# Chunked attention and a snake MLP: V loads of one batch split in two, its last units reordered, and fewer output matmuls beside the attention

## The chip, the cores and the metric

The kernel runs on one core of one Trainium2 chip. A core has five engines with their own instruction streams: TensorE (PE in the profile; its weight loads are listed as PEld), VectorE (DVE), ScalarE (ACT), GpSimd (POOL) and SyncE (SP). They meet through semaphores. The metric is device time in microseconds (us) of one execution; less is better.

## The reference

Two stages run one after the other. The first is attention over chunks: 4 batches, 8 heads, 768 positions, head size 64. Each chunk of 32 queries sees its own 32 keys, 16 to the left, 8 to the right and 8 memory keys.

```python
chunk, left_ctx, right_ctx = (32, 16, 8)
for c in range(nc):
    q_c = q[:, :, c_start:c_end].copy()
    k_full = np.concatenate([mem_k, k_ctx], axis=2)
    v_full = np.concatenate([mem_v, v_ctx], axis=2)
    scores = scale * np.matmul(q_c, k_full.transpose(0, 1, 3, 2))
    scores = scores - np.max(scores, axis=-1, keepdims=True)
    a = np.exp(scores)
    a = a / (np.sum(a, axis=-1, keepdims=True) + 1e-09)
    out[:, :, c_start:c_end] = np.matmul(a, v_full)
```

The second is an MLP over the 3072 tokens with 512 features, 2048 hidden ones:

```python
h = x @ w_in
s = np.sin(alpha * h)
g = h + s * s / (alpha + 1e-09)
out = (g @ w_out)
```

## The kernel before, in words

Work is staged by batch. For each batch of 768 tokens there is an attention stage and an MLP pass, and the output product of a batch is spread over the stages that follow.

**Attention.** Three chunks are taken together, so a batch has 8 groups of 96 queries, and a tile of 96 queries sees 128 columns. `qk` makes the scores `sc` of four head pairs with 8 small matmuls, `exps` turns them into `pt` on ScalarE with 3 to 4 Exp instructions, `pv` multiplies by V into `ot` (8 matmuls) and normalizes on VectorE (`rinv`, then `x_blk`), and `xt` transposes `x_blk` (4 matmuls) and copies the result into `xT`, the input of the MLP.

**Batch 0** runs in `first_burst`, from a list written by hand, `ORDER`. In it "k n" and "q n" transpose a head pair, "s n" is `qk` of unit n, "e n" its exponentials, "v n" its `pv`, "x n" its `xt`, and "z n" is n matmuls of zeros. Unit n holds four query groups of head pair n // 2; so units 4 and 5 read V of heads 4 and 5, units 6 and 7 that of heads 6 and 7. For units 2 to 7 `xt` puts 2 matmuls of zeros (`spin`) ahead of its transposes. After the exponentials of unit 7, line 375 does a one-column Sin on ScalarE whose result nothing reads.

**Batches 1, 2 and 3** run in `burst(b, stream, shares, lag)`. Step s issues `qk` and `exps` of group s, `pv` of group s - lag and `xt` of group s - lag - 1. Between them the step takes `shares[s]` output matmuls from a `Stream`. The stream holds the output product `l2` of the batch before: 96 matmuls of 128x512, in 6 groups of 16 with one output tile each; after a group the tile is copied by `put_out` (VectorE or ScalarE in turn) and sent out. `take(n)` adds n to a debt; it stops after a finished group, and what is left of the debt is taken by the next call.

**The MLP pass** goes over 16 column blocks ft. `l1` makes `hT` with 8 matmuls, then Sin on ScalarE (`u`), a square `s` on ScalarE, VectorE or GpSimd by a string of letters (A, D, P), and `finish` adds both on VectorE into `gT`. In the pass of batch 0 the stream is empty; after it, 4 output matmuls and then 3 after each of eight transposed pieces run ahead of the attention of batch 1. In the passes of batches 1 and 2, 2 output matmuls are taken from the stream ahead of each ft from 1 on, in that of batch 3 it is 3; in batches 1 and 2 every second ft also transposes a piece of K or Q of the next batch (`tt_a`). What is still in the stream when the last pass ends is done there.

**Buffers.** PSUM has a pool `big` of 3 tiles (`sc`, `ot`, `hT` and some transposes) and a pool `smp` of 2 (`o`, `z`, `tt_a`). A new tile waits for the last reader of the one whose place it takes.

**Loads.** Q, K, V and the weights are issued on GpSimd's queue. [...] a DMA is issued only when the one eight before it has landed. `load_v(b, n0, n1)` issues four DMAs for heads n0 / 8 to n1 / 8: 48 + 48 rows, and the left and right neighbours of each query group. Batch 0's V goes in three calls: heads 0 and 1 (n 0 to 16), heads 2 and 3, and heads 4 to 7; the weights `w_in` (four DMAs), K and Q of batch 1 and `w_out` follow.

Of the kernel before, what the change touches and what calls it, by code (L numbers as in the profile page):

```python
# [12 lines left out]
KW = 856  # L13
ORDER = (
    "k 0,q 0,memk 0,memv 0,k 1,s 0,e 0,z 1,s 1,e 1,q 1,k 2,s 2,e 2,s 3,v 0,q 2,e 3,k 3,x 0,v 1,q 3,s 4,e 4,x 1,"
    "s 5,e 5,z 1,v 2,s 6,e 6,z 2,v 3,x 2,v 4,s 7,e 7,x 3,v 5,x 4,v 6,x 5,v 7,x 6,x 7"
)
BF = mybir.dt.bfloat16
F32 = mybir.dt.float32
ACTF = mybir.ActivationFunctionType  # L20
# [29 lines left out]
def kernel(  # L50
# [12 lines left out]
    nc = tc.nc  # L63
# [25 lines left out]
    rows = consts.tile([P, 6], F32, name="rows")  # L89
# [36 lines left out]
    def load_v(b, n0, n1):  # L126


        vw = vws[b % 2].rearrange("p h j c -> p (h j) c")
        vf = v[b].rearrange("h s d -> (h s) d")  # L130
        vf = vf.rearrange("(n p) d -> p n d", p=QW)
        parts = (
            (vw[16:64, n0:n1, 0:D], vf[0:48, n0:n1]),
            (vw[72:120, n0:n1, 0:D], vf[48:96, n0:n1]),
            (vw[0:16, n0 + 1:n1, 0:D], vf[80:96, n0:n1 - 1]),
            (vw[120:128, n0:n1 - 1, 0:D], vf[0:8, n0 + 1:n1]),
        )
        for dst, src in parts:
            nc.gpsimd.dma_start(dst, src)  # L139
# [14 lines left out]
    zeros = consts.tile([P, 512], BF, name="zeros")  # L154
    nc.vector.memset(zeros[:], 0.0)  # L155

    def spin(n, z=None):

        if z is None:
            z = smp.tile([P, 512], F32, name="z", tag="sm")  # L160
        for _ in range(n):
            nc.tensor.matmul(z[:], zeros[:, 0:P], zeros[:])  # L162
# [26 lines left out]
        out=biasm[:], in0=rows[:, 0:5], scalar1=1.0, scalar2=-NEG, op0=ALU.subtract, op1=ALU.mult)  # L189
    nc.scalar.copy(memk_bf[:], memk_f[:])  # L190
    load_v(0, 16, 32)
    load_v(0, 32, 64)
    with nc.allow_non_contiguous_dma(reason="alpha transpose load"):
        nc.sync.dma_start(alpha_sb[:], moe_alpha.rearrange("(ft p) -> p ft", p=P))

# [81 lines left out]
    def exps(cells, sc):  # L277
        pt = pts[state["n"] % NPT]
        state["n"] += 1
        for m in range(3):  # L280
            cols = [((1 if j == 0 else 0), 4, (2 if j == NJ - 1 else 3))[m] for _, j in cells]
            c0 = 0
            for c1 in range(1, 5):
                if c1 < 4 and cols[c1] == cols[c0]:
                    continue
                nc.scalar.activation(  # L286
                    pt[:, 0:H * QW].rearrange("p (g e c) -> p e g c", g=4, e=2)[:, :, c0:c1, 32 * m:32 * m + 32],
                    sc[:, :, 0:4 * QW].rearrange("p g (e c) -> p g e c", e=4)[:, :, c0:c1, 32 * m:32 * m + 32],
                    ACTF.Exp, bias=biasm[:, cols[c0]:cols[c0] + 1], scale=0.125,
                )  # L290
                c0 = c1
        return pt
# [17 lines left out]
        )  # L310
        return x_blk, ot

    def xt(dst, x_blk, ot, copy=nc.vector.tensor_copy):
        if ot is None:
            z = smp.tile([P, 512], F32, name="z", tag="sm")
            spin(2, z)
            xtp = z[:].bitcast(BF)[:, 0:KT * QW]
        else:
            xtp = ot[:].bitcast(BF)[:, 0, 640:640 + KT * QW]
        xtp = xtp.rearrange("p (k c) -> p k c", k=KT)  # L320
        for kt in range(KT):
            nc.tensor.transpose(  # L322
                xtp[:, kt, :], x_blk[:, 2 * kt:2 * kt + 2, :].rearrange("p e d -> p (e d)"), ident[0:QW, 0:QW]
            )
        copy(dst, xtp)
# [4 lines left out]
    def burst(b, stream, shares, lag):  # L330

        xT = xp.tile([P, KT, S], BF, name="xT")
        ptl, xbl = {}, {}
        for s in range(NJ + lag + 1):
            n = shares[s] if s < len(shares) else 0
            if s < NJ:
                ptl[s] = exps(row(s), qk(row(s)))
            stream.take(n // 3, True)
            if 0 <= s - lag < NJ:
                xbl[s - lag] = pv(b, row(s - lag), ptl.pop(s - lag))  # L340
            stream.take((n + 1) // 3, True)
            if 0 <= s - lag - 1 < NJ:
                j = s - lag - 1
                xt(xT[:, :, QW * j:QW * j + QW], *xbl.pop(j))
            stream.take((n + 2) // 3, True)
        return xT

    def first_burst(kq):

        xT = xp.tile([P, KT, S], BF, name="xT")  # L350
        cells = [[(u // 2, 4 * (u % 2) + c) for c in range(4)] for u in range(8)]
        scl, ptl, xbl = {}, {}, {}
        for what, n in [t.split() for t in ORDER.split(",")]:
            n = int(n)
            if what == "k":
                t_k(kq[0], n)
            elif what == "q":
                t_q(kq[1], n, nc.vector.tensor_copy if n == 1 else nc.scalar.copy)
            elif what == "memk":
                mt = smp.tile([P, HP, 32], BF, name="mt", tag="sm")  # L360
                for hp in range(HP):
                    nc.tensor.transpose(
                        mt[:, hp, :],
                        memk_bf[0:32, 2 * hp:2 * hp + 2, :].rearrange("p e d -> p (e d)"),
                        ident[0:32, 0:32])
                nc.vector.tensor_copy(memkT[:], mt[:])
                put_memk(0)
            elif what == "memv":
                put_memv(0)
            elif what == "s":  # L370
                scl[n] = qk(cells[n])
            elif what == "e":
                ptl[n] = exps(cells[n], scl.pop(n))
                if n == 7:
                    nc.scalar.activation(rows[:, 0:1], zeros[:, 0:1], ACTF.Sin)
            elif what == "z":
                spin(n)
            elif what == "v":
                x_blk, ot = pv(0, cells[n], ptl.pop(n))
                xbl[n] = x_blk, (ot if n < 2 else None)  # L380
            elif what == "x":
                hf = n % 2
                xt(xT[:, n // 2, HALF * hf:HALF * hf + HALF].rearrange("p (k c) -> p k c", k=KT),
                   *xbl.pop(n), nc.scalar.copy if n in (4, 5, 6) else nc.vector.tensor_copy)
        return xT


# [106 lines left out]
    stream = Stream()  # L494
    xT = first_burst(kq)
# [3 lines left out]
    for i in range(B):  # L499
        gT = gp.tile([P, FT, S], BF, name="gT")  # L500
        last = i == B - 1
        at_ft = {2 * n: n for n in range(8)}
        pieces = []
        if not last:
            srcs = [(kq_next[n % 2], n // 2) for n in range(2 * HP)]
        state["pools"] = 1

        def pair_to(n):
            while len(pieces) < min(n, 2 * HP):
                pieces.append(pair_up(*srcs[len(pieces)], nc.vector.tensor_copy if i == 0 and len(pieces) in (2, 4, 6) else None))  # L510

        def piece(n):
            pair_to(n + 3)
            (t_k if n % 2 == 0 else t_q)(pieces[n], n // 2)

        if 0 < i < B - 1:
            pair_to(2)
        finish, late = None, None
        for ft in range(FT):
            sq = ("DADPADAPADAPDAAA" if i == 0 else "ADAAPDADADAPADAD")[ft]  # L520
            if 1 <= ft:
                stream.take(3 if last else 2)
            if 0 < i < B - 1 and ft in at_ft:
                piece(at_ft[ft])
            if i == 0 and ft == 8:
                pair_to(2)
            if i == 0 and ft == 13:
                load_v(1, 0, H * NJ)
            if finish is not None and ft - 1 == 11 and i == 0:
                late = finish  # L530
            elif finish is not None:
                finish()
                if late is not None:
                    late()
                    late = None
            finish = l1(i, ft, xT, gT, sq, i == 0 and ft in (3, 7, 11))
        finish()
        stream.add(l2(i, gT, last))
        if not last:
            if i == 0:  # L540
                state["pools"] = 0
                stream.take(4)
                for n in range(2 * HP):
                    piece(n)
                    stream.take(3, True)
                put_memv(1)
            if i + 2 < B:
                kq_next = load_qk(i + 2)
            if i == 0:
                xT = burst(i + 1, stream, (5, 5, 5, 4, 4, 4, 4, 4, 3, 3, 3, 3), 3)  # L550
            else:
                xT = burst(i + 1, stream, (16, 8, 6, 6, 6, 5, 5, 5, 5, 5), 1)
            if i + 2 < B:
                put_memk(i + 2)
            stream.take(3)
            if i + 2 < B:
                load_v(i + 2, 0, H * NJ)
                put_memv(i + 2)
# [31 lines left out]
```

The softmax here doesn't subtract the row's maximum and nothing guards it: scores larger than these inputs give would overflow.

## Time and profile before

The median of five runs is 233.96 us (233.74 to 234.1). The profiled execution took 234.1 us, and its span from the first to the last instruction is 232.3 us.

| Stage (us from the span's start) | length | PE busy | DVE busy | ACT busy |
|---|---|---|---|---|
| load and attention of batch 0 (0 to 27.8) | 27.8 | 23.3 | 18.4 | 17.3 |
| MLP pass of batch 0 (27.8 to 50) | 22.2 | 21.2 | 18.7 | 18.4 |
| transposes for batch 1 (50 to 59.5) | 9.5 | 9.0 | 8.4 | 5.0 |
| attention of batch 1 (59.5 to 78.3) | 18.8 | 17.9 | 12.9 | 14.4 |
| MLP pass of batch 1 (78.3 to 107) | 28.7 | 27.7 | 24.6 | 22.9 |
| attention of batch 2 (107 to 128.7) | 21.7 | 21.3 | 14.1 | 14.0 |
| MLP pass of batch 2 (128.7 to 158.5) | 29.8 | 29.0 | 24.9 | 24.1 |
| attention of batch 3 (158.5 to 179.8) | 21.3 | 21.0 | 13.4 | 13.4 |
| MLP pass of batch 3 (179.8 to 211.4) | 31.6 | 30.0 | 22.2 | 21.6 |
| output of batch 3 (211.4 to 232.3) | 20.9 | 17.7 | 2.5 | 1.5 |

Busy time is the time in which the engine had an instruction under way. Matmuls are pipelined, so PE counts as busy although it may issue less than it could. An engine's share is an average over stages; what bounds a stage is read from the wait that ends last in it.

### The profile page before, as it was taken

The numbers are of one execution on the slowest core, as the hardware profiler recorded it, in microseconds if no ns is written. First come the engines' busy times: TensorE is split into PE (matmuls) and PEld (weight loads), VectorE is DVE, ScalarE is ACT, GpSimd is POOL, SyncE is SP. The second block draws the span as 40 slices with busy tenths as digits, with TensorE's granted clock in tenths as the row PEclk, the third lists the DMA queues.
The fourth block names the chain that finished last, engine by engine and source line by source line (L and its number), as shares of the span: only waits on it lengthen the run. The fifth ranks groups of instructions, "written<-read, shape, count | busy, mean of one in ns | idle before, by whom it ended". The sixth has DMA issues, their size and how long they took to land.

```text
span 232.3 us, 4566 instructions
## 1 busy us (share of the span) xinstructions
PE 217.9 (94%) x1813; PEld 123.1 (53%) x1842; DVE 160.1 (69%) x288; ACT 152.6 (66%) x246; POOL 69.5 (30%) x80
## 2 busy tenths in 40 slices
PE   7996899989989999999999999998999999899994
PEld 2454565555446565654555656564555555453453
DVE  5675679888657897988467798887565368774110
ACT  3487789884887387898564877878664676880110
POOL 8898312595912115157300315020000020110000
PEclk9999999999999999999999999999999999999999
DMA  6999999999999910109995101010111010101112
GB/s 83 149 175 151 206 204 206 208 156 91 146 235 168 88 45 0 48 5 175 172 142 90 45 0 48 0 45 3 45 48 57 36 47 0 45 0 48 71 66 90
DMA packets 51805, 21.13 MB, mean 91 GB/s; under 512 B 36296, under 2 KB 48840, under 8 KB 51784
## 3 DMA queue, kind: packets, MB, share of 16 engines
q0 software_dynamic: 45568, 14.41, 76.1%
q1 hardware_dynamic: 6216, 6.43, 9.4%
q8 instruction: 14, 0.23, 0.4%
q14 instruction: 7, 0.06, 0.1%
HBM read 28.94 MB, written 6.29 MB: 152 GB/s over the span
## 4 chain that ended last, share of the span: by engine, by line
PE 61%; ACT 12%; DVE 9%; DMA 8%; issue 6%; POOL 2%; POOLq 1%; DVEq 0%; ACTq 0%
PE o L479 27%; PE hT L400 21%; DMA q_bf<-in_q_dram 5%; DVE gT L429 5%; ACT u L412 4%; PE ot L301 3%; ACT pt L286 3%; DMA vw<-in_v_dram 2%; PE sc L270 2%; DVE s L421 2%; ACT s L415 2%; PE tt_a L242 2%; PE ot L322 2%; PE o L468 2%; PE o L449 1%
## 5 line engine op out<-in xcount | busy, mean ns | idle before, releaser
L400 PE MATMUL hT<-xT,w_in_sb 128*128 128x384 bf16 x488 | 87.1, 326 | 3.0 <-DVE gT L429 2.8
L479 PE MATMUL o<-w_out_sb,gT 128*128 128x512 bf16 x313 | 84.9, 380 | 1.8 <-issue 0.5
L429 DVE SCALAR_TENSOR_TENSOR gT<-s,inv_alpha,hT 128x768 bf16<-128x768 f32 x61 | 61.0, 1012 | 19.7 <-ACT s L415 11.2
L412 ACT ACTIVATE u<-hT,alpha_sb 128x768 f32<-128x768 f32 x61 | 54.8, 898 | 24.5 <-PE hT L400 23.5
L400 PEld LDWEIGHTS <-w_in_sb 128*128 128x128 bf16 x512 | 49.3, 98 | 37.5 <-issue 3.8
L286 ACT ACTIVATE pt<-sc,biasm 128x256 bf16<-128x256 f32 (+2 forms) x104 | 39.1, 471 | 15.4 <-PE sc L270 15.4
L479 PEld LDWEIGHTS <-gT 128*128 128x128 bf16 x336 | 29.3, 98 | 24.3 <-DVE gT L429 1.2
L417 POOL TENSOR_TENSOR s<-u 128x768 f32<-128x768 f32 x9 | 13.2, 1466 | 87.5 <-ACT u L412 61.3
L415 ACT ACTIVATE s<-u 128x768 f32<-128x768 f32 x32 | 27.0, 844 | 1.0
L421 DVE TENSOR_TENSOR s<-u 128x768 f32<-128x768 f32 x23 | 24.3, 1056 | 2.3 <-ACT u L412 2.2
L306 DVE TENSOR_TENSOR x_blk<-ot,rinv 96x512 bf16<-96x512 f32 x32 | 22.0, 686 | 1.1
L139 POOL DMA_DIRECT2D vw<-in_v_dram x24 | 22.0, 924 | 0.6 <-DMA q_bf<-in_q_dram 0.5
L216 POOL COPY pr<-q_bf 128x768 bf16<-128x768 bf16 x12 | 10.8, 897 | 34.3 <-PE tt_a L242 24.4
L437 DVE COPY o_sb<-o 128x512 f32<-128x512 f32 x12 | 8.3, 689 | 15.6 <-PE o L479 15.5
L437 ACT COPY o_sb<-o 128x512 f32<-128x512 f32 x11 | 6.4, 584 | 17.9 <-PE o L479 17.9
L305 DVE RECIPROCAL rinv<-ot 96x8 f32<-96x8 f32 x32 | 6.4, 201 | 16.5 <-PE ot L301 16.3
L301 PEld LDWEIGHTS <-pt 128*128 128x128 bf16 x256 | 11.7, 97 | 7.5 <-issue 3.0
L301 PE MATMUL ot<-vw,pt 128*128 128x65 bf16 x256 | 13.0, 193 | 2.3 <-DMA vw<-in_v_dram 1.1
L162 PE MATMUL z<-zeros 128*128 128x512 bf16 x36 | 12.6, 451 | 2.1 <-DVE zeros L155 1.2
L242 PEld LDWEIGHTS <-pr 128*128 128x128 bf16 x144 | 10.0, 98 | 5.9 <-DVE pr L216 0.9
L270 PEld LDWEIGHTS <-kTi 64*128 64x128 bf16 x256 | 6.8, 94 | 11.3 <-PE ot L322 5.5
L322 PEld LDWEIGHTS <-x_blk 96*128 96x128 bf16 x128 | 8.7, 97 | 7.3 <-DVE x_blk L306 1.5
(76 smaller groups left out, 169.8 us busy)
## 6 DMA issues: line engine op xcount, KB each, us to landing
out_dram<-o_sb SPq DMA_DIRECT2D x23, 256.0 KB, 2.4
k_bf<-in_k_dram POOLq DMA_DIRECT2D x3, 768.0 KB, 8.7
q_bf<-in_q_dram POOLq DMA_DIRECT2D x3, 768.0 KB, 12.4
vw<-in_v_dram POOLq DMA_DIRECT2D x6, 384.0 KB, 15.0
w_in_sb<-in_moe_w_in_dram POOLq DMA_DIRECT2D x4, 512.0 KB, 9.7
w_out_sb<-in_moe_w_out_dram POOLq DMA_DIRECT2D x2, 1024.0 KB, 24.1
k_bf<-in_k_dram POOLq DMA_DIRECT2D x4, 192.0 KB, 5.1
q_bf<-in_q_dram POOLq DMA_DIRECT2D x4, 192.0 KB, 5.6
```

The lines of the kernel that those rows point to most:

```text
L139: nc.gpsimd.dma_start(dst, src)
L242: nc.tensor.transpose(t[:, r, :], src[:, r].rearrange("p e d -> p (e d)"), ident[:])
L286: nc.scalar.activation(pt[:, 0:H * QW].rearrange("p (g e c) -> p e g c", g=4, e=2)[:, :, c0:c1, 32 * m:32 * m + 32], sc[:, :, 0:4 * QW].re ...
L301: nc.tensor.matmul(otv[:, n // 4, n % 4, :], pt[:, QW * n:QW * n + P], vws[b % 2][:, 2 * hp + n % 2, j, 0:D + 1])
L306: nc.vector.tensor_tensor(out=x_blk[:].rearrange("p (g e) d -> p g e d", g=2), in0=otv[0:QW, :, :, 0:D], in1=rv.unsqueeze(3).to_broadcast( ...
L400: nc.tensor.matmul(hts[hf][:, 0:HALF], w_in_sb[:, kt, P * ft:P * ft + P], xT[:, kt, HALF * hf:HALF * hf + HALF], start=(kt == 0), stop=(kt ...
L412: nc.scalar.activation(u[:], hT[:, :, 0:HALF], ACTF.Sin, scale=alpha_sb[:, ft:ft + 1])
L415: nc.scalar.activation(s2[:], u[:], ACTF.Square)
L421: nc.vector.tensor_tensor(out=s2[:], in0=u[:], in1=u[:], op=ALU.mult)
L429: nc.vector.scalar_tensor_tensor(out=gv, in0=s2[:], scalar=inv_alpha[:, ft:ft + 1], in1=hT[:, :, 0:HALF], op0=ALU.mult, op1=ALU.add)
L437: (nc.vector.tensor_copy if s % 2 == 0 else nc.scalar.copy)(o_sb[:], o[:])
L479: nc.tensor.matmul(o[:], gT[:, ft, P * s:P * s + P], w_out_sb[:, ft, :], start=(ft == 0), stop=(ft == FT - 1),)
```

## The change

It does five things. (1) V of heads 4 to 7 of batch 0 is loaded by two calls, each of four DMAs, in place of one. (2) In `ORDER`, "s 7,e 7" stands ahead of "v 4". (3) `xt` puts 2, 2, 1, 1, 0, 0 matmuls of zeros ahead of the transposes of units 2 to 7 in place of 2 each, and the copy of unit 3 into `xT` is on ScalarE, not on VectorE. (4) The Sin of line 375 is gone. (5) The shares of the output matmuls in the attention of batches 1, 2 and 3 are smaller.

```diff
-    "s 5,e 5,z 1,v 2,s 6,e 6,z 2,v 3,x 2,v 4,s 7,e 7,x 3,v 5,x 4,v 6,x 5,v 7,x 6,x 7"
+    "s 5,e 5,z 1,v 2,s 6,e 6,z 2,v 3,x 2,s 7,e 7,v 4,x 3,v 5,x 4,v 6,x 5,v 7,x 6,x 7"
...
-    load_v(0, 32, 64)
+    load_v(0, 32, 48)
+    load_v(0, 48, 64)
...
-    def xt(dst, x_blk, ot, copy=nc.vector.tensor_copy):
+    def xt(dst, x_blk, ot, copy=nc.vector.tensor_copy, warm=0):
...
-            spin(2, z)
+            spin(warm, z)
...
                 ptl[n] = exps(cells[n], scl.pop(n))
-                if n == 7:
-                    nc.scalar.activation(rows[:, 0:1], zeros[:, 0:1], ACTF.Sin)
...
-                   *xbl.pop(n), nc.scalar.copy if n in (4, 5, 6) else nc.vector.tensor_copy)
+                   *xbl.pop(n), nc.scalar.copy if n in (3, 4, 5, 6) else nc.vector.tensor_copy,
+                   (0, 0, 2, 2, 1, 1, 0, 0)[n])
...
-                xT = burst(i + 1, stream, (5, 5, 5, 4, 4, 4, 4, 4, 3, 3, 3, 3), 3)
+                xT = burst(i + 1, stream, (5, 5, 4, 4, 4, 3, 3, 3, 3, 3, 2, 2), 3)
             else:
-                xT = burst(i + 1, stream, (16, 8, 6, 6, 6, 5, 5, 5, 5, 5), 1)
+                xT = burst(i + 1, stream, (16, 8, 6, 5, 5, 5, 5, 5, 4, 4), 1)
```

## The prediction

> **What bounds the kernel now.** The page's first part gives PE 217.9 of 232.3 us. Its fourth part, the chain that ended last, says who sets the end:
>
> ```profile
> PE 61%; ACT 12%; DVE 9%; DMA 8%; issue 6%; POOL 2%; POOLq 1%; DVEq 0%; ACTq 0%
> ```
>
> So an output matmul moved costs nothing only where it goes into a stretch in which PE is not that 61%. I went through the stages in order of time. First the chain in batch 0 (start, length, what):
>
> ```profile
> 10.31 6.18 DMA q_bf<-in_q_dram
> ...
> 16.77 5.67 DMA vw<-in_v_dram
> ...
> 22.58 0.40 PE ot L301 x8
> ...
> 23.30 1.36 ACT pt L286 x4
> ...
> 24.67 1.28 ACT L375
> ...
> 26.17 0.38 ACT xT L325
> ```
>
> The last V piece lands at 22.44; only then run v 4, s 7 behind it, e 7, the unused Sin's table load, and the xT copies on ACT; the MLP's first matmul is at 27.79. Who holds V back stands in POOL's timeline (start, length, idle before and its releaser):
>
> ```profile
> 11.13 5.14 POOL L139 DMA_DIRECT2D vw<-in_v_dram  x7
> 16.77 0.69 POOL L139 DMA_DIRECT2D vw<-in_v_dram  x1 [0.50 <-DMA q_bf<-in_q_dram]
> 17.84 3.01 POOL L202 DMA_DIRECT2D w_in_sb<-in_moe_w_in_dram  x4 [0.38 <-DMA vw<-in_v_dram]
> ```
>
> POOL issues one DMA per 0.6 to 0.75 us and waits for the DMA eight before. The issues by size and time to landing, in narrow windows, give
>
> ```profile
> vw<-in_v_dram POOLq DMA_DIRECT2D x1, 31.0 KB, 5.7
> vw<-in_v_dram POOLq DMA_DIRECT2D x1, 15.0 KB, 4.8
> w_in_sb<-in_moe_w_in_dram POOLq DMA_DIRECT2D x1, 512.0 KB, 6.6
> ```
>
> Then a step of batch 2's attention, on PE:
>
> ```profile
> 117.08 0.34 PE L270 MATMUL sc<-qT,kTi 64*128 64x96 bf16 x8
> 117.36 0.60 PE L479 MATMUL o<-w_out_sb,gT 128*128 128x512 bf16 x2
> 118.26 0.38 PE L479 MATMUL o<-w_out_sb,gT 128*128 128x512 bf16 x1
> 118.65 0.60 PE L479 MATMUL o<-w_out_sb,gT 128*128 128x512 bf16 x2
> ```
>
> PE has no gap over 0.1 us, ACT idles 0.4 to 0.9 us per step for sc: PE-bound. Last, the end of batch 3's pass, where the stream is empty:
>
> ```profile
> 201.48 0.89 ACT L412 ACTIVATE u<-hT,alpha_sb 128x768 f32<-128x768 f32 x1
> 202.44 1.47 POOL L417 TENSOR_TENSOR s<-u 128x768 f32<-128x768 f32 x1 [11.25 <-ACT u L412]
> 203.95 1.01 DVE L429 SCALAR_TENSOR_TENSOR gT<-s,inv_alpha,hT 128x768 bf16<-128x768 f32 x1 [1.09 <-POOL s L417]
> 205.01 2.81 PE L400 MATMUL hT<-xT,w_in_sb 128*128 128x384 bf16 x16 [0.27 <-DVE gT L429]
> ```
>
> Here PE waits for ACT, POOL and DVE in turn, through the hT buffers.
>
> [...] the trace agrees (5 o in 1.08 us of the chain, 0.216 each). [...] the page here shows PEclk 9 in all slices. [...] The trace is higher, 4.3 us for the first 192 KB and 4.8 for 15 KB with others in flight; I use the trace.
>
> **The change part by part.**
>
> *Split V.* The four DMAs of heads 4 and 5 go out at 13.79, 14.5, 15.2 and, since the fourth waits for Q's landing as now, 16.77. It carries 15 KB with half the V ahead of it: 4.8 to 5.7 us, landing 21.6 to 22.4, so v 4 gains 0.1 to 0.9. Heads 6 and 7 take w_in's place at 17.84, and at 0.73, 0.73 and 0.58 us per issue the last starts at 19.88; with 4.3 to 5.7 it lands at 24.2 to 25.6. I take 4.8, since less is queued ahead: v 6 starts at V = 24.75, against 24.65 now. The unknown is V.
>
> *Order.* s 7 follows x 2 at 21.5 instead of 22.91; its sc buffer is free. e 7 then ends near 23.3, not 24.66, so nothing waits on ACT after V.
>
> *After V.* x 5 (1 zero matmul), v 7 at V + 0.62; x_blk of 7 ends at V + 2.22 (rinv 0.2 and x_blk 0.69 twice on DVE, at today's offsets); x 7 at V + 2.35, the MLP at V + 2.52 = 27.27. Now it is V + 3.14, for the 0.69 wait for ACT and the zeros. The table load goes between x 6's copy (ends V + 2.35) and the first Sin: ends V + 3.65, and hT is complete at V + 3.98. Hidden; uncovered it would cost 1.28. First Sin: 28.8, not 29.30. **-0.5**; ends -1.0 (V 24.2) and +0.35 (V 25.6). The copy of unit 3 on ACT falls behind e 7, where ACT is idle. Six zero matmuls fewer (1.3 us) leave PE a gap of about 1 us near 24[...].
>
> The first w_in goes out at 20.5 instead of 17.84. At 6.6 us it would land at 27.1, just in time. Later loads slip by about 2 us: batch 1's K and Q (now 36.4 and 40.2; copied at 41.4 and 42.1, no one waiting before 50), w_out (45.3 for 50.2), V of batch 1 (60.5 for 64.7): slack. The pass of batch 0 follows ACT (16 Sins at 0.90 and 8 squares at 0.84 are 21.1 of the 22.9 us from the first Sin to the last square's end at 52.2), so it hands the gain on.
>
> *Batch 1.* The stream gives 6 matmuls fewer to the attention (47 to 41), and the pass gets them behind ft 9, 10 and 11 (18 to 24). From the table load at 60.51 the attention is ACT's: five Exp sets end at 67.87, then each step is sc to Exp to sc, 1.68 us, with PE equally full; last comes DVE at 1.11 us per group. So only about 0.25 of the 1.30 is got. In the pass DVE has a backlog from 94 to 110.2; the later hT of ft 12 (+0.87) delays its Sin, its square and the gT of ft 12 and 13, and the next sc waits for the latter: 107.2 instead of 106.7. **+0.25** together.
>
> *Batch 2.* By the order of instructions the attention has 64 instead of 70: -6 x 0.216 = -1.30, all PE-bound (shortest step 1.88, over ACT's 1.68). The pass has 32 instead of 26: 2 more behind ft 0, 2 each behind ft 13 and 14. The first cost 0.43; at the end PE now idles 0.58 for gT, which takes in most of the rest; next sc +0.64. **-0.65**. The 64th output copy now comes at the attention's very end; with the V memory cast 0.61 and the table load 1.28 the first Sin is 0.9 late, but hT 3 needs its gT 0.9 us after that is ready.
>
> *Batch 3.* Again -1.30. In the pass 2 more after ft 0, 1 more after ft 8, 3 more after ft 9. Sin 10 has to wait for hT 10, which comes 1.3 later, less ACT's queue: Sin 11 +1.2, POOL's square, gT 11, hT 14, gT 15 at 212.4 instead of 211.4: +1.03. **-0.27**; were the tail fully bound by PE it would be 0, with full cover -0.8.
>
> Sum: -0.5 + 0.25 - 0.65 - 0.27 = -1.17. The span 232.3 becomes 231.1, the profiled execution 234.1 becomes 232.9; the median, 0.14 lower, 232.8. Matmul records are partly missing and each tail was walked by hand, so I state 232.9.
>
> **Rivals.**
> A. The passes take back all that the attentions give. For it: batches 1 to 3 move 18 matmuls, 3.9 us, and PE's real slack at the ends of the three passes is only about 0.55, 0.58 and 0.88 us of named waits. Against: the pass of batch 1 has room for more fill, since DVE sets its end. With batch 0 also even (V at 25.3): 233.9.
> B. Slower: the first w_in lands late. Four more issues ahead of it on POOL put it at 20.5. For it: the four w_in DMAs took 6.6 to 12.5 us, median 9.7; at 9.7 it lands at 30.2 and the MLP starts 2.4 late instead of 0.5 early, all else as above: 235.7. Against: the long ones queued behind each other, the first took 6.6 with all of V ahead of it. It decides from a landing of 28.9 on (27.8 plus the 0.67 of batches 1 to 3 plus 0.47).
> C. More is won: V lands at 24.2 and the tails hide more (batch 1 at 0, batch 3 at -0.8): -1.0 - 0.65 - 0.8 = -2.45, 231.5.
> That the change does not do what it says is excluded by the order of instructions.
>
> **How the numbers follow.** Forecast 0.53, A 0.22, B 0.13, C 0.12. The forecast's own range is 232.2 to 233.6, from V (0.9 us wide) and 0.4 for each tail. For 8 in 10 I cut half of B and part of C: 231.7 to 234.6. A difference of 0.2%, 0.47 us, is about what this kernel's measurement can tell. Faster: 0.85 of the forecast, C and a little of A, 0.58; same: the rest of the forecast and most of A, 0.24; slower: B and some of A, 0.18.
>
> **What would show it.** First hT near 27.3 with v 6 waiting for vw until about 24.8; w_in not named as a releaser of PE; the attentions of batches 2 and 3 shorter by 1.3 each and that of batch 1 by 0.1 to 0.4; passes of batches 2 and 3 longer by 0.6 and 1.0; the table load ended before the first hT. The forecast is wrong if v 6 waits past 25.3, if hT waits for w_in, if PEclk dips below 9 before 30 us, or if the passes grow by 1.3 each.

## The result and the profile after

The changed kernel takes 236.82 us, median of 27 runs (233.92 to 239.74), against 233.97 us, median of 48 runs (233.16 to 234.81) of the kernel before. The medians differ by 2.85 us, 1.2%; the ratio is 1.006 (95% interval 1.0045 to 1.0075), and it is smaller than that of the medians because it leaves out the executions more than 1.5% above the fastest. The forecast was 232.9 us with a range up to 234.6: the change makes the kernel slower, not faster.

The times of after lie in steps, by the mean granted TensorE clock of the execution: ten runs with 1.0 take 233.92 to 235.84 us, ten with 0.993 take 236.16 to 238.52, five with 0.986 take 238.77 to 239.74; three in between, with 0.998 or 0.999, take 234.87 to 236.59 (28 executions: one of 235.84 us is listed with its clock besides the 27). A clock of 1.0 is full speed; in the trace of before, which has 0.998, the clock falls only in the last microsecond of the span, to 0.50 from 231.56 us on. The 13 executions with 0.998 or more have a median of 235.44 us, so after is 1.5 us slower than before even at full clock. The profiled execution took 238.52 us, span 236.7, clock 0.993.

The page of after: the chain's shares by engine, and the row of the granted clock in 40 slices of 5.9 us, in tenths of full speed (9 is 90% or more).

```profile
PEclk9999979999999999999999999999999999999999
PE 54%; DVE 12%; ACT 11%; DMA 9%; issue 7%; POOL 4%; POOLq 1%; DVEq 0%; ACTq 0%
```

Before, PE had 61% of the chain and DMA 8%. The 7 in the clock's row is the slice from 29.6 to 35.5 us. Now the chain of batch 0 (start, length, what):

```profile
10.09 7.04 DMA q_bf<-in_q_dram
17.13 0.28 issue
17.41 3.24 POOL vw L139 x5
20.65 8.04 DMA w_in_sb<-in_moe_w_in_dram
28.69 0.05 issue
28.74 5.70 PE hT L400 x24
```

Where it had run over V, v 4, e 7, the Sin's table load and the xT copies, it now runs from Q's landing over POOL's issues to the first w_in. POOL's timeline of after (start, length, idle before and its releaser):

```profile
10.93 4.68 POOL L139 DMA_DIRECT2D vw<-in_v_dram  x7
17.41 3.25 POOL L139 DMA_DIRECT2D vw<-in_v_dram  x5 [1.80 <-DMA q_bf<-in_q_dram]
20.65 3.03 POOL L203 DMA_DIRECT2D w_in_sb<-in_moe_w_in_dram  x4
```

and the issues from 16 to 24 us by size, number and time to landing:

```profile
vw<-in_v_dram POOLq DMA_DIRECT2D x2, 96.0 KB, 3.2
vw<-in_v_dram POOLq DMA_DIRECT2D x2, 15.0 KB, 3.1
vw<-in_v_dram POOLq DMA_DIRECT2D x1, 30.0 KB, 4.2
```

V is in sooner than forecast: the last piece, issued at about 20, landed near 24. These short landings fall where the DMA engines moved little: in the table of stretches 34 GB/s from 18 to 20 us, where before they moved 126. PE's timeline shows what it then waited for:

```profile
26.28 0.34 PE L323 MATMUL z<-ident,x_blk 96*128 96x96 bf16 x4 [0.49 <-DVE x_blk L307]
28.74 5.70 PE L400 MATMUL hT<-xT,w_in_sb 128*128 128x384 bf16 x24 [2.12 <-DMA w_in_sb<-in_moe_w_in_dram]
```

x 7 is done at 26.6 and the MLP could start. It waits 2.12 us for w_in, and then 24 matmuls take 5.5 us up to the next ones, which before took 3.91. The same 5.6 us in the table of stretches (PE, PEld, DVE, ACT, POOL busy; PEclk; DMA share; GB/s):

```profile
28.70:34.30 5.60, 5.56 (x25) 2.90 (x26) 1.73 (x2) 1.99 (x3) 0.00 (x0) 0.70 1.25 205
```

So of the 2.58 us that batch 0 loses, 0.95 is the later start (28.74 for 27.79) and 1.62 the lowered clock (5.53 for 3.91). Later stages run at full clock (1.00 from 32.09 to 230 us), and their lengths can be compared. An attention is counted from its Exp table load (batch 1) or its first scores to the next hT 0, a pass from there to the next first scores, the last one to the first output matmul after gT 15:

| us | before | after | difference | forecast |
|---|---|---|---|---|
| load, batch 0, transposes (to the table load) | 60.51 | 63.09 | +2.58 | -0.5 |
| attention 1 | 17.65 | 18.07 | +0.42 | -0.25 |
| pass 1 | 28.53 | 29.16 | +0.63 | +0.5 |
| attention 2 | 21.92 | 20.86 | -1.06 | -1.30 |
| pass 2 | 29.50 | 30.95 | +1.45 | +0.64 |
| attention 3 | 21.58 | 20.66 | -0.92 | -1.30 |
| pass 3 | 31.75 | 33.04 | +1.29 | +1.03 |

The last six rows come to +1.81, where the forecast had -0.67. A step of batch 2's attention, beside that shown of before:

```profile
120.48 0.34 PE L271 MATMUL sc<-qT,kTi 64*128 64x96 bf16 x8
120.76 0.39 PE L479 MATMUL o<-w_out_sb,gT 128*128 128x512 bf16 x1
120.99 0.41 PE L302 MATMUL ot<-vw,pt 128*128 128x65 bf16 x8
121.45 0.38 PE L479 MATMUL o<-w_out_sb,gT 128*128 128x512 bf16 x1
121.66 0.34 PE L323 MATMUL ot<-ident,x_blk 96*128 96x96 bf16 x4
121.83 0.60 PE L479 MATMUL o<-w_out_sb,gT 128*128 128x512 bf16 x2
122.36 0.34 PE L271 MATMUL sc<-qT,kTi 64*128 64x96 bf16 x8
```

PE still has no named wait and the step takes 1.88 us, as forecast. Elsewhere there are waits that the kernel before does not have. VectorE and PE in batch 1's attention:

```profile
70.10 0.69 DVE L307 TENSOR_TENSOR x_blk<-ot,rinv 96x512 bf16<-96x512 f32 x1
70.70 0.68 DVE L437 COPY o_sb<-o 128x512 f32<-128x512 f32 x1
71.30 0.34 DVE L326 COPY xT<-ot 128x384 bf16<-128x384 bf16 x1
```

```profile
71.70 0.40 PE L302 MATMUL ot<-vw,pt 128*128 128x65 bf16 x8 [0.78 <-DVE xT L326]
```

The copy of an output group (`put_out`, line 437) has come between x_blk and the copy into xT, so xT, the ot buffer that it frees and the next weighted sum are late. Before, that copy stood ahead of a group's reciprocal, in a gap of VectorE, and PE's wait for xT was 0.2 us:

```profile
66.44 0.69 DVE L437 COPY o_sb<-o 128x512 f32<-128x512 f32 x1 [0.41 <-PE o L479]
67.27 0.20 DVE L305 RECIPROCAL rinv<-ot 96x8 f32<-96x8 f32 x1
```

The same kind of wait for xT, 0.24 us each, stands at 127.03 and 178.98 in the attentions of batches 2 and 3. In the pass of batch 2 it is the transposes of the next K:

```profile
147.27 0.49 PE L243 MATMUL tt_a<-ident,pr 128*128 128x128 bf16 x6 [0.64 <-DVE o_sb L437]
```

`tt_a` and `o` share the two tiles of `smp`; one holds the new group, the other is still to be copied out.

The end of batch 3's pass of after, PE alone:

```profile
207.07 1.46 PE L400 MATMUL hT<-xT,w_in_sb 128*128 128x384 bf16 x8 [0.30 <-DVE gT L429]
...
209.40 2.76 PE L400 MATMUL hT<-xT,w_in_sb 128*128 128x384 bf16 x16 [0.88 <-DVE gT L429]
...
215.83 0.61 PE L479 MATMUL o<-w_out_sb,gT 128*128 128x512 bf16 x2 [0.43 <-DVE gT L429]
```

It is the forecast's chain, with hT 14 waiting for gT.

### The profile page after: what moved, and what is told of

Its sections match the earlier page's. It is cut to its first block, busy times and chain, and to the rows that moved or that the text cites. A ratio compares the mean times of both kernels' runs of the same rounds, so it can differ in the third digit from the quotient of the medians.

```text
span 236.7 us, 4562 instructions
## 1 busy us (share of the span) xinstructions
PE 218.3 (92%) x1806; PEld 122.6 (52%) x1836; DVE 159.3 (67%) x287; ACT 153.4 (65%) x246; POOL 71.3 (30%) x84
## 4 chain that ended last, share of the span: by engine, by line
PE 54%; DVE 12%; ACT 11%; DMA 9%; issue 7%; POOL 4%; POOLq 1%; DVEq 0%; ACTq 0%
PE o L479 23%; PE hT L400 20%; DMA q_bf<-in_q_dram 5%; DVE gT L429 4%; ACT u L412 4%; DMA w_in_sb<-in_moe_w_in_dram 3%; ACT s L415 3%; DVE s L421 3%; PE ot L302 3%; DVE x_blk L307 2%; ACT pt L287 2%; PE sc L271 2%; PE tt_a L243 2%; PE o L468 1%; PE ot L323 1%
## 5 line engine op out<-in xcount | busy, mean ns | idle before, releaser
L400 PE MATMUL hT<-xT,w_in_sb 128*128 128x384 bf16 x488 | 89.2, 330 | 4.4 <-DMA w_in_sb<-in_moe_w_in_dram 2.1
L412 ACT ACTIVATE u<-hT,alpha_sb 128x768 f32<-128x768 f32 x61 | 54.8, 899 | 25.9 <-PE hT L400 24.8
L400 PEld LDWEIGHTS <-w_in_sb 128*128 128x128 bf16 x512 | 49.8, 99 | 40.2 <-issue 5.2
L479 PEld LDWEIGHTS <-gT 128*128 128x128 bf16 x336 | 29.9, 98 | 24.9 <-DVE gT L429 1.4
L421 DVE TENSOR_TENSOR s<-u 128x768 f32<-128x768 f32 x23 | 23.8, 1035 | 5.6 <-ACT u L412 5.5
L139 POOL DMA_DIRECT2D vw<-in_v_dram x28 | 24.0, 868 | 1.8 <-DMA q_bf<-in_q_dram 1.8
L217 POOL COPY pr<-q_bf 128x768 bf16<-128x768 bf16 x12 | 10.3, 861 | 36.0 <-PE tt_a L243 25.3
L162 PE MATMUL z<-zeros 128*128 128x512 bf16 x30 | 10.6, 451 | 1.4 <-DVE zeros L155 1.2
## 6 DMA issues: line engine op xcount, KB each, us to landing
w_out_sb<-in_moe_w_out_dram POOLq DMA_DIRECT2D x2, 1024.0 KB, 25.9
```

The lines of the kernel that those rows point to most:

```text
L400: nc.tensor.matmul(hts[hf][:, 0:HALF], w_in_sb[:, kt, P * ft:P * ft + P], xT[:, kt, HALF * hf:HALF * hf + HALF], start=(kt == 0), stop=(kt ...
L412: nc.scalar.activation(u[:], hT[:, :, 0:HALF], ACTF.Sin, scale=alpha_sb[:, ft:ft + 1])
L421: nc.vector.tensor_tensor(out=s2[:], in0=u[:], in1=u[:], op=ALU.mult)
L479: nc.tensor.matmul(o[:], gT[:, ft, P * s:P * s + P], w_out_sb[:, ft, :], start=(ft == 0), stop=(ft == FT - 1),)
```

## The experiments

The theory after the result had three parts: the reordered end of batch 0 wins about 1 us; the new shares cost 1.8; the split of V puts w_in behind four more issues, so that it can come late, and PE's clock falls for a while beside the wait. Rivals are named with each run. Each kernel was measured beside the kernel before, whose median was 233.83 to 233.90 us in these series.

**One load.** The changed kernel with V of heads 4 to 7 in one call again.

```diff
-    load_v(0, 32, 48)
-    load_v(0, 48, 64)
+    load_v(0, 32, 64)
```

> The changed kernel with V of heads 4 to 7 in one call of four DMAs again. Theory (the four extra V issues let the DMA queue run dry and put the first w_in 4.3 us later; PE then idles 2.1 us and its clock halves for a while): the first w_in lands near 24.4, PE does not wait for it, the first hT starts near 26.7 (22.58 for v 4 plus 4.1 as in the changed kernel), PEclk stays 9 in every slice, and the times lie within 1 us of each other. With the moved output matmuls still costing 1.8: 234.6 us. Rival (the missing zero matmuls let the clock drop, whatever V does): PEclk falls below 9 near 26 to 32 us in this one too, 236 to 237 us with a scatter of some us.

234.93 us (234.33 to 235.53, 7 runs), ratio 1.0046 (1.0028 to 1.0064). The first w_in goes out at 17.96, the MLP starts at 27.05 without a wait, the clock is 1.0 in every run. So, with the rest of the change in place, it is the split that brings the wait and the scatter, 1.9 us of the median. Most of that is the lowered clock: after's executions at full clock are 0.5 us above this run. What is left is slower than before by 1.1, and from the Exp table load of batch 1 to the output of batch 3 it takes 152.72 us instead of 150.93: the shares.

**Split alone.** The kernel before with the split load and nothing else of the change.

```diff
-    load_v(0, 32, 64)
+    load_v(0, 32, 48)
+    load_v(0, 48, 64)
```

> The kernel before with V of heads 4 to 7 in two calls and nothing else. Theory: the first w_in is issued near 20.6 and lands near 28.5, PE waits about 1 us for it, and the clock is at risk; 235 to 236.5 us. Rival (the split is harmless by itself, since the zero matmuls keep the clock up and the old order wants w_in only at 27.8): 233.7 to 234.4 us.

234.13 us (232.96 to 235.39, 14 runs), ratio 1.0001 (0.9983 to 1.0019). The rival held: with the old order the split costs nothing in the median, and the clock is 0.998 or more in all runs. In its trace Q landed earlier, w_in went out at 19.58 and the MLP started at 26.75 without a wait. So the split harms together with the new order. That this is because the new order brings PE to the MLP earlier while w_in comes later is argued: in this one trace Q was early, and w_in with it.

**Shares alone.** The kernel before with the new shares.

```diff
-                xT = burst(i + 1, stream, (5, 5, 5, 4, 4, 4, 4, 4, 3, 3, 3, 3), 3)
+                xT = burst(i + 1, stream, (5, 5, 4, 4, 4, 3, 3, 3, 3, 3, 2, 2), 3)
...
-                xT = burst(i + 1, stream, (16, 8, 6, 6, 6, 5, 5, 5, 5, 5), 1)
+                xT = burst(i + 1, stream, (16, 8, 6, 5, 5, 5, 5, 5, 4, 4), 1)
```

> The kernel before with the new shares of output matmuls in the attention of batches 1 to 3 and nothing else. Theory (read from the changed kernel's stages: batch 1 +1.05, batch 2 +0.2, batch 3 +0.55): 235.7 us. Rival (the prediction's sum, +0.25 - 0.65 - 0.27): 233.3 us.

235.87 us (234.58 to 236.31, 6 runs), ratio 1.0075 (1.0051 to 1.0099), as the theory had it. The stages of batches 1 to 3 lose 1.04, 0.38 and 0.37 us, as in the changed kernel to 0.01, and PE's waits in them (engine, line, releaser: total, times, longest, from 59 to 160 us) are those found there:

```profile
PE ot L301 <- DVE xT L325: 1.0, 2, 0.8
PE tt_a L242 <- DVE o_sb L437: 0.6, 1, 0.6
```

**Old shares.** The changed kernel with the shares of before.

```diff
-                xT = burst(i + 1, stream, (5, 5, 4, 4, 4, 3, 3, 3, 3, 3, 2, 2), 3)
+                xT = burst(i + 1, stream, (5, 5, 5, 4, 4, 4, 4, 4, 3, 3, 3, 3), 3)
...
-                xT = burst(i + 1, stream, (16, 8, 6, 5, 5, 5, 5, 5, 4, 4), 1)
+                xT = burst(i + 1, stream, (16, 8, 6, 6, 6, 5, 5, 5, 5, 5), 1)
```

> The changed kernel with the old shares of output matmuls; only the end of batch 0 is changed against the kernel before. Theory: 1.8 us less than the changed kernel, so a median near 235.0, with the same scatter of about 6 us and PEclk below 9 after the wait for w_in. Rival (the prediction's sum for the shares): 0.7 us more than the changed kernel, near 237.5.

233.22 us (232.19 to 237.68, 8 runs), ratio 0.9947 (0.9928 to 0.9967). Five runs with clock 1.0 take 232.19 to 233.54, three with 0.985 to 0.993 take 235.82 to 237.68. The theory's median of 235.0 missed, since five of the eight kept the clock; its scatter came. The stages from batch 1 on have the lengths of before to 0.02 us. In the profiled execution PE waited 1.34 us for w_in:

```profile
28.70 5.66 PE L400 MATMUL hT<-xT,w_in_sb 128*128 128x384 bf16 x24 [1.34 <-DMA w_in_sb<-in_moe_w_in_dram]
```

The scatter is batch 0's and does not need the shares. At full clock the five runs have a median of 232.72 us, no more than the order alone, which is the next run: in those executions the split costs nothing that shows.

**Order alone.** The previous kernel with one load too: the new `ORDER`, six zero matmuls fewer, no Sin, unit 3's copy on ScalarE.

```diff
-    load_v(0, 32, 48)
-    load_v(0, 48, 64)
+    load_v(0, 32, 64)
...
-                xT = burst(i + 1, stream, (5, 5, 4, 4, 4, 3, 3, 3, 3, 3, 2, 2), 3)
+                xT = burst(i + 1, stream, (5, 5, 5, 4, 4, 4, 4, 4, 3, 3, 3, 3), 3)
...
-                xT = burst(i + 1, stream, (16, 8, 6, 5, 5, 5, 5, 5, 4, 4), 1)
+                xT = burst(i + 1, stream, (16, 8, 6, 6, 6, 5, 5, 5, 5, 5), 1)
```

> V of heads 4 to 7 in one load and the shares of before; the order, the missing Sin, the fewer zero matmuls and unit 3's copy on ScalarE stay. Theory (late w_in, cold PE and dearer shares are the whole loss, the reordered attention of batch 0 is a gain): the first w_in goes out at about 18, PE does not wait for it, the granted clock stays 1.0, the MLP starts near 27.0, 0.7 us before that of before, and the time is 232.8 to 233.3 us, below before. Rival (the order brings nothing, since the pass of batch 0 takes it back): 233.7 to 234.1, as before.

232.86 us (232.48 to 233.45, 11 runs), ratio 0.9943 (0.9925 to 0.9962): it is faster than both kernels. PE's timeline:

```profile
22.50 0.40 PE L301 MATMUL ot<-vw,pt 128*128 128x65 bf16 x8
...
26.43 0.34 PE L322 MATMUL z<-ident,x_blk 96*128 96x96 bf16 x4 [0.49 <-DVE x_blk L306]
26.61 4.07 PE L399 MATMUL hT<-xT,w_in_sb 128*128 128x384 bf16 x24
```

From v 4 to the MLP it takes 4.11 us, before 5.21 (22.58 to 27.79). From the MLP's start to batch 1's table load it is 32.73 us, before 32.72: what the order wins is handed on whole.

**Zeros back.** The kernel with the old shares, and the six zero matmuls in their places again; the split stays.

```diff
-                   (0, 0, 2, 2, 1, 1, 0, 0)[n])
+                   (0, 0, 2, 2, 2, 2, 2, 2)[n])
```

> The changed kernel with the shares of before and the six zero matmuls back, two ahead of the transposes of each of units 2 to 7; the split load and the new order stay. Theory 1 (PE's clock falls because PE has been little busy for the last microseconds before the wait and idle in it): the zeros fill that stretch, the granted clock stays 1.0 or falls less often, and the highest times go from 237.7 down to 235 or less, though PE may still wait up to 1.3 us for w_in; median 233.2 to 233.8. Theory 2 (the wait for w_in alone decides the clock): clocks of 0.993 and 0.986 and times over 235.5 appear as with the shares of before alone.

233.97 us (231.82 to 236.67, 22 runs), ratio 0.998 (0.9958 to 1.0001). Six of 22 runs have a clock of 0.991 to 0.993, five of them at 235.89 to 236.67. Theory 1 falls in its forecast: zeros ahead of the wait do not always keep the clock. The execution that was profiled had full clock and no wait for w_in, so the executions with the low clock have no trace. No run was at 0.986, against one of eight with the old shares, which is too few to say that they do nothing.

**Zeros in the wait.** The kernel with the old shares and the changed kernel's zeros, with nine zero matmuls more between the last transposes and the first hT.

```diff
-    "s 5,e 5,z 1,v 2,s 6,e 6,z 2,v 3,x 2,s 7,e 7,v 4,x 3,v 5,x 4,v 6,x 5,v 7,x 6,x 7"
+    "s 5,e 5,z 1,v 2,s 6,e 6,z 2,v 3,x 2,s 7,e 7,v 4,x 3,v 5,x 4,v 6,x 5,v 7,x 6,x 7,z 9"
```

> The changed kernel with the shares of before, and nine zero matmuls (1.94 us at 0.216 each) between the last transposes of batch 0 and its first MLP matmul, that is in the place in which PE waits for w_in. Theory (the high times are PE's lowered clock, not the wait): granted clock 1.0 in every run, no time above 235, first MLP matmul near 28.5 to 29 whether w_in is there or not; median 233.3 to 234.3. Rival (the high times come from w_in landing even later in some executions): times above 236 stay, with the clock at 1.0.

234.64 us (233.93 to 235.51, 22 runs), ratio 1.0023 (1.0007 to 1.0038). The times over 235.6 are gone, though five are above the theory's 235, and the clock is 0.998 or more in 21 of 22 runs. So the high times were the lowered clock and not w_in landing later still: the rival falls. In the one run with 0.993, which is the profiled one, the clock was at half speed from 19.6 to 23 us (0.50 from 20 to 22 us in the table of stretches), ahead of the zeros and of any wait for w_in. The median misses the theory by 0.3: it is 1.4 us over that of the old shares, and 1.9 over the five runs of that kernel at full clock, which is what nine zero matmuls take (1.94 us from the first of them to hT in the trace). Where w_in is in time they delay the MLP.

**w_in first.** The kernel with the old shares, and the first w_in issued between the two halves of the split.

```diff
     load_v(0, 32, 48)
+    load_w_in(0, 512)
     load_v(0, 48, 64)
...
-    for c0, c1 in ((0, 512), (512, 1024), (1024, 1536), (1536, 2048)):
+    for c0, c1 in ((512, 1024), (1024, 1536), (1536, 2048)):
```

> The changed kernel with the shares of before and the first w_in issued between the two halves of the split V load, so ahead of the V of heads 6 and 7. Theory (w_in is late because of its place behind four more issues, after a stall for Q has let the DMA queue run dry): w_in goes out near 18.5 to 19.5 us instead of 20.9, lands by 26.5, PE does not wait for it and no time over 235 is left; the V of heads 6 and 7, now behind 512 KB, comes 0.8 to 2 us later and PE waits for it instead; median 233.0 to 234.2. Rival (after the dry stretch the first 512 KB come late wherever they stand): PE still waits for w_in and times over 235.8 remain.

235.84 us (234.15 to 237.28, 9 runs), ratio 1.0091 (1.006 to 1.0123). Neither held as written. w_in went out at 17.43, landed 5.8 us later, and PE did not wait for it: that part of the theory stands. But the V of heads 6 and 7, behind 512 KB, came so late that PE waited for it, and the clock was at 0.984 to 0.993 in seven of nine runs. PE's timeline, and the table of stretches as above:

```profile
25.73 0.40 PE L303 MATMUL ot<-vw,pt 128*128 128x65 bf16 x8 [2.09 <-DMA vw<-in_v_dram]
```

```profile
26.00:28.00 2.00, 1.58 (x22) 1.09 (x18) 1.74 (x4) 0.78 (x2) 1.34 (x2) 0.56 1.24 205
```

So the clock fell after a gap in which PE waited for V, as it did beside one for w_in; the same table has 0.50 from 28 to 32 us, and the first 24 hT matmuls took 6.21 us, where before they took 3.91.

**Group end.** The kernel before with the new shares, batch 1's in another shape: the same sum, but the second output group ends one output matmul earlier in its step, as before the change.

```diff
-                xT = burst(i + 1, stream, (5, 5, 4, 4, 4, 3, 3, 3, 3, 3, 2, 2), 3)
+                xT = burst(i + 1, stream, (5, 5, 5, 4, 4, 3, 3, 3, 3, 2, 2, 2), 3)
```

> The kernel before with the new shares, as in the run of the shares alone (235.87 us), but batch 1's shares are 5,5,5,4,4,3,3,3,3,2,2,2: the same sum 41, with the second output group ending one output matmul earlier in its step, as it does before. Theory (the new shares cost more because an output copy on VectorE falls between x_blk and xT): the wait of 0.8 us for xT in batch 1's attention is gone, that attention takes 18.4 to 18.6 us and the time is 235.2 to 235.5. Rival (the number of matmuls moved decides, not where the copies fall): attention of batch 1 at 18.7 to 19.1 and 235.8 to 236 us.

235.13 us (234.77 to 235.68, 17 runs), ratio 1.0047 (1.0034 to 1.0061), 0.74 below the shares alone and just under the theory's range. From the first scores on, batch 1's attention takes 18.38 us; it is 18.57 before and 18.98 with the shares alone. VectorE's timeline:

```profile
66.21 0.69 DVE L437 COPY o_sb<-o 128x512 f32<-128x512 f32 x1 [0.41 <-PE o L479]
67.04 0.20 DVE L305 RECIPROCAL rinv<-ot 96x8 f32<-96x8 f32 x1
67.28 0.69 DVE L306 TENSOR_TENSOR x_blk<-ot,rinv 96x512 bf16<-96x512 f32 x1
67.89 0.34 DVE L325 COPY xT<-ot 128x384 bf16<-128x384 bf16 x1
```

The copy is back in the gap, and the wait for xT is gone. So 0.6 us of batch 1's 1.05 is the place of one copy. The pass keeps its +0.63.

**Two fewer, two more.** The order alone, with two output matmuls fewer or more in the attention of batches 2 and 3 (the change takes six).

```diff
-                xT = burst(i + 1, stream, (16, 8, 6, 6, 6, 5, 5, 5, 5, 5), 1)
+                xT = burst(i + 1, stream, (16, 8, 6, 6, 6, 5, 5, 5, 4, 4), 1)
```

> The kernel with the new order alone (one V load, batch 1's shares as before) and two output matmuls fewer in the attention of batches 2 and 3, 16,8,6,6,6,5,5,5,4,4: a third of the change's six, with the groups that end in the attention at the same places as before and the fifth ahead of hT 6. Theory (the change's cost in batches 2 and 3 comes from copies of output groups in bad places): no wait of PE for xT or for an output copy; each attention 0.4 us shorter, each pass 0.1 to 0.4 longer; 232.5 to 232.9 us. Rival (the passes are simply full, each matmul costs more there than it saves): passes 0.5 to 0.6 longer each, 233.0 to 233.3 us.

```diff
-                xT = burst(i + 1, stream, (16, 8, 6, 6, 6, 5, 5, 5, 5, 5), 1)
+                xT = burst(i + 1, stream, (16, 8, 6, 6, 6, 6, 6, 5, 5, 5), 1)
```

> As that kernel, but two output matmuls more than before in the attention of batches 2 and 3, 16,8,6,6,6,6,6,5,5,5. Theory: each attention 0.4 us longer, PE being its bound, each pass 0 to 0.4 shorter: 232.9 to 233.6 us. Rival (the passes are full, so taking matmuls out of them wins more than it costs): passes 0.5 to 0.6 shorter each and 232.4 to 232.7 us.

Two fewer: 232.63 us (232.43 to 233.52, 6 runs), ratio 0.9955 (0.994 to 0.9969). Two more: 232.74 us (232.07 to 233.25, 6 runs), ratio 0.9952 (0.9935 to 0.997). Against the order alone (232.86) both are within what a measurement can tell. The stages say why:

| difference from the order alone, us | attention 2 | pass 2 | attention 3 | pass 3 |
|---|---|---|---|---|
| two fewer | -0.43 | +0.32 | -0.22 | +0.43 |
| two more | +0.27 | -0.36 | +0.28 | -0.32 |

A matmul moved costs in the pass about what it saves in the attention. The theory of the two fewer had that nearly right, but it missed a wait of PE for an output copy in pass 2 (0.4 us, once):

```profile
PE o L478 <- DVE o_sb L436: 0.4, 1, 0.4
```

With two more each attention lost 0.27, not 0.4, so that the total is just under the theory's range; the rival's 0.5 to 0.6 per pass did not come.

## Why the prediction was wrong

**The parts add up.** The order alone is 1.0 us below the kernel before, the shares are 1.8 by the stages and 2.0 by their run, and going from one load to the split adds 1.9 to the median under the new order: +2.7 to +2.9, against +2.85 measured.

**Split V: sooner than priced, and not what mattered.** V was forecast in at 24.75, with v 6 waiting for it; v 6 ran at 24.00 without a wait, and x 7 was done at 26.6, where the MLP had been forecast at 27.27. Three of the named signs of a wrong forecast came: hT waited for w_in, the clock fell before 30 us, and the passes of batches 2 and 3 grew by 1.45 and 1.29.

**First w_in: the step that failed first.** "At 6.6 us it would land at 27.1, just in time". The issue time was right (20.5 forecast, 20.65 measured), the duration was not: 8.0 us, landing at 28.69. It was taken from one landing in one execution, and with the price on the edge any excess went straight to the path. Over the five traces with w_in behind the split V (after, split alone, old shares, zeros back, zeros in the wait), its first landing took 5.4 to 8.0 us and came at 25.5 to 28.7; in three with V in one load (before, one load, order alone) it took 6.6 to 6.8 and came at 24.3 to 24.7. So the duration is no mark of the split; what differed in all five was the start, 19.58 to 20.94 for 17.49 to 17.96, and it was the start that used up the margin: begun at before's 17.84, a load of 8.0 us would have been in at an estimated 25.9, ahead of the end of x 7 at 26.6. This was rival B's mechanism, just short of the landing of 28.9 that was named as its point of decision. B priced the late start alone: 0.95 later here, not its 2.4.

The stall is part of the late start. Batch 0's last Q piece took 7.04 us in the profiled execution of after and POOL stood 1.80 us for it, up to 17.41; from 18 to 20 us the DMA engines moved 34 GB/s. This varies between executions of one order: in the split alone the same wait was 0.2 us. Why w_in then takes between 5.4 and 8.0 us was not settled; the shortest, of the zeros back, came after a stall of 1.21 us.

**The clock: the larger miss in batch 0.** "Six zero matmuls fewer (1.3 us) leave PE a gap of about 1 us near 24". That such a gap does the clock no harm was the author's estimate; the trace of before has one of 1.12 us, ahead of v 4, up to 22.58, with the clock at 1.00. The gap near 24 was no trouble; the gap that counted was the one at 26.6, where PE stood for 2.12 us. The clock fell to half (0.50) late in gaps of 2.12 (after) and 1.34 us (old shares), and 0.5 us after one of 2.09 (w_in first). Executions of one kernel differ: after shows 1.0, 0.993 and 0.986. Nor does the length of a gap decide: in the trace of after PE also waited 1.32 us for an Exp, up to 19.85, and the clock stayed at 1.00.

The record of the clock in the traces shows what goes with a fall. In after the clock stood at 0.50 from 28.67 to 32.08 us, 3.41 us long; in w_in first it was lowered for about twice that. The table has PE's busy time in the 3.41 us that end where the clock falls. Falls at the very end, where the output runs out, are left out (in before at 231.56 us).

| run | clock falls at, us | PE busy in the 3.41 us before |
|---|---|---|
| after | 28.67 | 0.69 |
| old shares | 28.55 | 1.48 |
| w_in first | 26.26 | 1.32 |
| zeros in the wait | 19.57 | 2.12 |

Two stretches of this length in after, in the table's form as above, the second of them the one before the fall. Of the other stretches, counted off in such lengths from the fall over the span, the first is the least busy that left the clock full:

```profile
18.43:21.84 3.41, 2.06 (x36) 1.38 (x32) 1.38 (x5) 3.41 (x13) 3.41 (x6) 1.00 1.22 80
25.26:28.67 3.41, 0.69 (x8) 0.40 (x8) 1.53 (x6) 1.97 (x3) 1.94 (x3) 1.00 1.23 200
```

In after the clock fell behind the stretch in which PE did least; in w_in first, where it fell behind 1.32 us of work, a stretch with 2.23 (16.02 to 19.43) left it full. So in these two traces what went with a fall was how little PE did within 3.41 us, not one gap. The gap of 1.34 us in the old shares lay in a stretch with 1.48 us of work, the one of 1.32 us in after in a stretch with 2.06. No threshold follows: 2.12 us was too little in one trace and 2.06 enough in another. Why one kernel's clock falls in some executions and not in others was not shown, since after has one trace.

A difference of 0.007 in the mean clock is 1.66 us of a 236.7 us span, close to the 1.62 us that one lowered stretch cost in the trace. No execution of after with 0.986 has a trace; w_in first, with 0.984, shows a stretch about twice as long. Filling the gap with zeros ends the high times (none over 235.51 us in 22 runs); that removing the six zeros caused them was not borne out. The gap is not the only way to a fall: in the zeros in the wait the clock fell at 19.6 us with no gap over 0.6 us (the longest from 10 us on was 0.54), and among 59 runs of the kernel before three were at 235.69 to 236.31 us with 0.985 to 0.993. Why those three fell is open, since none of them has a trace.

**After V, Order: right in what waits, and undersized.** The table load lay hidden (26.32 to 27.60 in after), nothing waited for ACT after V, and in the order alone the pass of batch 0 handed the gain on whole. The forecast had -0.5 because it put V of the last heads at 24.75; in the order alone V is in by 22.5 with one load, and from v 4 on 1.1 us is won. The gain was the order's, not the split's.

**Batch 1: +0.25 forecast, +1.05 measured.** With the copy in its old place it is +0.45: the attention -0.18 (forecast -0.25), the pass +0.63 (+0.5), with the wait for gT that was named. The forecast counted the matmuls that moved. It did not follow where the groups of 16 then end, and so where VectorE's 0.68 us copy falls: 0.6 us.

**Batch 2: -0.65 forecast, +0.39 measured.** The attention misses by 0.24, its wait for xT behind a copy. The pass misses by 0.81: 0.64 is the wait of `tt_a` for a tile that the copy holds, and the slack of 0.58 at the end did not take in the rest. **Batch 3: -0.27 forecast, +0.37 measured.** Again 0.24 of the attention's 0.38 is that wait. The pass was right in its chain, Sin 11, POOL's square, gT 11, hT 14, and 0.26 short. The place of a copy was put to an experiment in batch 1 alone; in batches 2 and 3 they are read from the waits, and the remaining 0.56 us of the two misses is not assigned.

**Rival A** said that the passes take back all that the attentions give. It had the direction: they take back more, +3.37 for -1.56 over the three batches. The two runs with two matmuls fewer or more show the exchange at about even; of the 1.8 us that the new shares lose, 0.6 is shown to be the place of a copy, and 1.1 more is read from the waits behind copies.

## What to carry to other kernels

When a stream of small work is spread over other work by counts, follow where its groups end and which engine then copies what: a 0.7 us copy between two links of a chain cost 0.6 us in one attention, more than the 0.18 that moving six matmuls had won there. Issues moved ahead of a load can cost the load its margin even when they free something else: here four of them put w_in at 20.65 for 17.84. A landing priced "just in time" should be priced from several executions (this one took 5.4 to 8.0 us over five traces), with what stands behind it, here the clock. What a gap cost in clock did not follow from its length alone: the clock fell in one of 1.34 us, with 1.48 us of PE work in the 3.41 us before the fall, and stayed full through one of 1.32 us in a stretch with 2.06. Keeping the order, the fewer zeros, the copy and the missing Sin, and dropping the split and the shares, makes 232.86 us, 0.6% below the kernel before (ratio 0.9943).

## What the runs showed of the hardware

TensorE's granted clock fell to half (0.50) late in gaps of 2.12 us (after, at 28.67) and 1.34 us (old shares, at 28.55), 0.5 us after one of 2.09 us (w_in first, at 26.26), and once with no gap over 0.6 us (zeros in the wait, at 19.57); it stayed at 1.00 through one of 1.32 us (after, up to 19.85) and one of 1.12 us (before, up to 22.58). In the 3.41 us before those falls PE was busy for 0.69 to 2.12 us. The clock stayed lowered for 3.41 us in after and for about twice that in w_in first. The gaps of after and the old shares were for w_in, that of w_in first for V. With nine matmuls of zeros in the gap the clock stayed at 0.998 or more in 21 of 22 runs and fell in the other ahead of them; they cost 1.4 us of the median.

A 512 KB load issued behind small ones landed after 5.4 (zeros back) to 8.0 us (after) over five traces. V pieces of 15 to 96 KB issued from 17.41 to 20.65 us in after, where the DMA engines moved 34 GB/s from 18 to 20 us, landed after 2.3 to 4.2 us; in before one of 15 KB, the last of the V issues from 4.89 to 7.54 us, and one of 31 KB, issued at 16.77, landed after 4.8 and 5.7, where the DMA engines moved 102 GB/s from 5 to 7 us and 131 from 17 to 18.
